# One weight load moved to ScalarE's queue, and two stores moved ahead of GpSimd's casts, in a fused attention and feed-forward kernel

## The chip, the cores and the metric

The kernel runs on one core of a Trainium2 chip. The metric is the device time of one execution in microseconds. Before the change it was 313.09 us, the median of 3 runs (313.03 to 315.12). A profiled execution of the same kernel spans 312.8 us on the core.

The core has five engines with an instruction stream each: TensorE (PE in the profile, its weight loads PEld), VectorE (DVE), ScalarE (ACT), GpSimd (POOL) and SyncE (SP). [...] Transfers between HBM and the core's memory are issued from SyncE's, ScalarE's or GpSimd's stream and carried out by 16 DMA engines.

## The reference, cut to what matters

Sliding-window attention over 8 batches of 8 heads, 576 positions and 64 values per head, followed by two dense layers with a GELU between them. All inputs and the output are float32; the kernel computes in float16 and accumulates in float32.

```python
def attention(q, k, v):                      # (8, 8, 576, 64) each
    scores = q @ k.transpose(0, 1, 3, 2) / 8.0
    pos = np.arange(576)
    mask = np.abs(pos[:, None] - pos[None, :]) <= 32
    scores = np.where(mask, scores, -1e9)
    attn = softmax(scores, axis=-1)          # exp(s - max) / (sum + 1e-9)
    return attn @ v

x = attention(q, k, v).transpose(0, 2, 1, 3).reshape(4608, 512)
h = x @ w_in                                 # (4608, 512) @ (512, 2048)
out = gelu_tanh(h) @ w_out                   # (4608, 2048) @ (2048, 512)
```

## The kernel before

The 4608 rows are worked on in 9 tiles of 512 (`t`), the attention in 8 batches (`b`). While the dense layers of tile `t` run, the attention of batch `t + 1` is woven between their matmuls. Batch 0 has no dense layer to hide behind, so its attention and the loading of the weights make up the start of the kernel.

The start: queries, keys and values of batch 0 are issued on SyncE (two transfers on ScalarE), and after them `w_in`, in four blocks of 512 columns with two halves each (512 KB per half). Of block 0, rows chunks 0 and 1 are the first half.

```python
    def load_w_in(i, w, c0=0, c1=4):
        nc.sync.dma_start(w[:, c0:c1, :], w_in_v[:, c0:c1, 512 * i:512 * i + 512])
        return w
    # ...
    load_table(exp_set)
    vs(4, 0, 1, 2, 3)                        # values of batch 0: tail, then 4 chunks
    wi = []
    for i in range(4):
        wi.append(stage_w())
        for c0 in (0, 2):
            load_w_in(i, wi[i], c0, c0 + 2)
```

The softmax's sums are inverted on ScalarE as exp(-ln(d)), once for each of four groups of heads in batch 0. The first weight block is cast to float16 by GpSimd, ScalarE and VectorE, and TensorE then begins the first dense layer.

```python
    def invert(b, g, d):
        # ... lt: a tile for the result
        nc.scalar.activation(lt[:, 0:n], d[:, 0:n], AF.Ln)
        nc.scalar.activation(lt[:, 0:n], lt[:, 0:n], AF.Exp, scale=-1.0)
        return lt
    # ...
    cast_v(0, 3, nc.vector.tensor_copy)                                       # values, last chunk
    nc.vector.tensor_copy(Vs[0][odd, 7, :, :], Vs[0][odd, 3, :, :])
    nc.scalar.copy(Vs[0][even, 6, :, :], raws[0][3][even, 3, :, :])           # ScalarE's part of it
    for g in range(4):
        times(0, g, os[g], groups.pop((0, g)), (3, 6, 7))                     # weights times values
        spread(0, g, os[g], lts[g])                                           # xT, by the inverted sums
    for c in range(4):
        cast_w(wi[0], w_in16[:, :, 0:512], (3,), (c,), (1,))
```

The end of tile 0: the second dense layer leaves four row blocks (`t4`) of 128 rows. Blocks 0 and 1 go into one tile `yo2`, blocks 2 and 3 into tiles of another pool. They aren't stored at once but put on a list, in the order 0, 3, 1, 2.

```python
        if fc == NF - 1:
            if "yo" not in pys:
                pys["yo"] = hp.tile([128, 2, 512], FP32, name="yo2", tag="qt16")
            yo = pys["yo"][:, t4, :] if t4 < 2 else yp.tile([128, 512], FP32, name="yo", tag="yo")
            (nc.scalar.copy if t4 > 1 else nc.vector.tensor_copy)(yo, pys[t4])
            later.append((t4, yo))
```

The tag `qt16` has one buffer. The next tile of that tag is the float16 tile for the query tails of batch 2, so the first copy into it has to wait until both blocks in `yo2` have been stored. (The profile shortens the tiles' names: `yo` stands for both kinds, and `qt<-qt` is the copy of query tails into `qt16`.)

```python
        def rest(i):                          # query and key tails of batch 2, on ScalarE
            qt16, kt16 = tails_of("q"), tails_of("k") if i == 4 else None
            if i < NPAIR:
                nc.scalar.copy(qt16[:, i, :, :, :].rearrange("p j h d -> p h j d"),
                               qt[:, 2 * i:2 * i + 2, :].rearrange("p h (j d) -> p h j d", j=4))
            # ... i == 3: transpose of the query tails; i == 4: key tails
```

The first dense layer of tile 1 has 16 columns of 128 features (`fc`), each with four matmuls (L530) and a GELU on ScalarE (L538). The stores, the casts of batch 2's values (`cast_v(2, c)`, on GpSimd) and the tail copies (`parts[1]`) stand between them. Three PSUM buffers hold the columns, so TensorE runs at most three columns ahead of the GELUs.

```python
            for fc in range(begun, NF):
                ffn_in(t, fc)                                   # 4 matmuls and the GELU
                if t == 1 and fc == 3:
                    parts[0]()                                  # keys of batch 2; loads of its values
                    combine(4, nc.vector)
                if t == 1 and fc in (5, 6):
                    store(0, *later.pop(0), slice(0, 512), nc.scalar)
                if t == 1 and 6 <= fc < 10:
                    cast_v(2, fc - 6)                           # GpSimd
                if t == 1 and fc == 7:
                    while later:
                        store(0, *later.pop(0))                 # GpSimd
                if t == 1 and 9 <= fc < 14:
                    parts[1](fc - 9)                            # ScalarE: tails
```

After this loop come the second dense layer of tile 1 and, between its matmuls, batch 2's scores, the pairing copies of its values on VectorE (`pair_v`), and the loads of batch 3.

Of the kernel before, what the change touches and what calls it, by code (L numbers as in the profile page):

```python
# [36 lines left out]
def cut(b):  # L37
    return 120 if b else 128
# [33 lines left out]
def kernel(  # L72
# [9 lines left out]
    nc = tc.nc  # L82
# [106 lines left out]
    def pair_v(b, copy, hs=slice(0, H)):  # L189

        V = Vs[b % 2]
        copy(V[64:128, 4:8, hs, :], V[64:128, 0:4, hs, :])
        copy(V[0:64, 4:7, hs, :], V[0:64, 1:4, hs, :])
# [8 lines left out]
    w_in_v = moe_w_in.rearrange("(c p) f -> p c f", p=128)  # L202
    w_out_v = moe_w_out.rearrange("(c p) f -> p c f", p=128)

    def stage_w():
        return stage.tile([128, 4, 512], FP32, name="wst", tag="stage")

    def load_w_in(i, w, c0=0, c1=4):
        nc.sync.dma_start(w[:, c0:c1, :], w_in_v[:, c0:c1, 512 * i:512 * i + 512])  # L209
        return w  # L210

    def load_w_out(i, w, c0=0, c1=4):
# [13 lines left out]
    qk(6)  # L226
    load_table(exp_set)
    vs(4, 0, 1, 2, 3)
    wi = []
    for i in range(4):  # L230
        wi.append(stage_w())
        for c0 in (0, 2):
            load_w_in(i, wi[i], c0, c0 + 2)

    idle = KTs[1][:, 0, 0:512]
    nc.vector.memset(idle, 0.0)
# [57 lines left out]
    def cast_v(b, c, copy=nc.gpsimd.tensor_copy):  # L294
        copy(Vs[b % 2][:, c, :, :], raws[b][3][:, c, :, :])
# [6 lines left out]
    def trans_tails(b, pt, half=slice(0, 128), copy=nc.vector.tensor_copy):  # L302
        t16 = halfs[b][2]
        for pr in range(NPAIR):
            nc.tensor.transpose(pt[:, pr, half], t16[half, 2 * pr:2 * pr + 2, :], idn[half, half])
        if half.stop > 64:
            copy(KLs[b % 2], pt[:, 0:4, 64:128])
        if half.start < 64:
            nc.vector.tensor_copy(QTs[b][:, :, :, 128:144],
                                  pt[:, 0:4, 0:64].rearrange("d r (p j) -> d r j p", j=4))  # L310
# [11 lines left out]
    def trans_out(b, pr, pt, ptk, copy=nc.vector.tensor_copy):  # L322
        nc.vector.tensor_copy(QTs[b][:, pr, :, 0:128], pt[:, 0:4, :])
        copy(
            KTs[b % 2][:, pr, :].rearrange("d (p j) -> d p j", j=4),
            ptk[:, 0:4, :].rearrange("d j p -> d p j"))
# [119 lines left out]
    def sum_up(b, g, d, pe):  # L446
        for h in range(2):
            nc.tensor.matmul(d[64 * h:64 * h + 64, 0:size(b, g)], ones, pe[:, h, :], start=True, stop=True)  # L448
# [15 lines left out]
    def weigh(b, g, pair=None):  # L464
        pe = groups.pop((b, g))
        if pair is not None:
            od = psS.tile([128, 2, 512], FP32, name="ps_od", tag=f"S{pair}")
            o, d = od[:, 0, :], od[:, 1, :]
        else:
            o = psO.tile([128, 512], FP32, name="ps_o", tag="O")  # L470
            d = psO.tile([128, 512], FP32, name="ps_d", tag="D")
        sum_up(b, g, d, pe)
        times(b, g, o, pe)
        return o, d

    def size(b, g):
        return 4 * cut(b) if g < 4 else 4 * NPAIR * (144 - cut(b))

    def invert(b, g, d):
        n = size(b, g)  # L480
        lt = ap_.tile([128, 512], FP32, name="lt") if b or g < 2 or g == 4 else \
            yp.tile([128, 512], FP32, name="lt0", tag="yo")
        nc.scalar.activation(lt[:, 0:n], d[:, 0:n], AF.Ln)  # L483
        nc.scalar.activation(lt[:, 0:n], lt[:, 0:n], AF.Exp, scale=-1.0)  # L484
        return lt

# [24 lines left out]
    def ffn_in(t, n, d0=0, d1=4, then=True):  # L511
        fc = column(t, n)
        if t not in gTs:
            gTs[t] = gp.tile([128, NF, 512], FP16, name="gT", tag="gT")
        if d0 == 0:
            if t == 0:
                i = n % 8
                if i in (4, 6):
                    phs["S"] = psS.tile([128, 2, 512], FP32, name="ph2", tag=f"S{i // 2 - 2}")
                phs[fc] = psO.tile([128, 512], FP32, name="ph", tag="DO"[i]) if i < 2 else \  # L520
                    bank(i - 2) if i < 4 else phs["S"][:, i % 2, :]
            else:
                i = 3 if n in (1, 2) else 0 if n == 0 else (2, 1, 0)[n % 3]
                if n == 1:
                    phs["S"] = psS.tile([128, 2, 512], FP32, name="ph3", tag="S0")
                phs[fc] = bank(i) if i < 2 else phs["S"][:, n - 1, :] if i == 3 else \
                    psO.tile([128, 512], FP32, name="ph", tag="D")
        ph = phs[fc]
        for dc in range(d0, d1):
            nc.tensor.matmul(ph, w_in16[:, dc, fc * 128:fc * 128 + 128],  # L530
                             xT[:, dc, t * 512 % RING:t * 512 % RING + 512],
                             start=(dc == 0), stop=(dc == 3))
        if d1 == 4 and then:
            gelu(t, n)

    def gelu(t, n):
        fc = column(t, n)
        nc.scalar.activation(gTs[t][:, fc, :], phs[fc], AF.Gelu_apprx_tanh)  # L538
        if t and n % 4 == 3:
            sums(t, n // 4)  # L540
# [20 lines left out]
    def combine(i, eng):  # L561
        dst, x, y = wino["todo"][i]
        eng.tensor_tensor(dst, x, y, op=ALU.subtract)
# [14 lines left out]
    def store(t, t4, yo, cols=slice(0, 512), *engs):  # L578

        m = i = 0  # L580
        while m < 128:
            b, c = divmod(t * 512 + t4 * 128 + m, S)
            q0, n = (0, cut(b)) if c < 4 * cut(b) else (cut(b), 144 - cut(b))
            j, p = divmod(c - 4 * q0, n)
            e = min(n - p, 128 - m)
            nj = 1 if p else max(1, min(4 - j, (128 - m) // n))
            eng = engs[i % len(engs)] if engs else nc.gpsimd
            if nj > 1:
                e = nj * n
                eng.dma_start(out_v[b, j:j + nj, q0:q0 + n, cols], yo[m:m + e, cols])  # L590
            else:
                eng.dma_start(out_v[b, j, q0 + p:q0 + p + e, cols], yo[m:m + e, cols])  # L592
            m += e
            i += 1

    later = []
# [84 lines left out]
    def pieces(tag, name):  # L681
        return psO.tile([128, 512], FP32, name=name, tag=tag) if tag in "OD" else \
            psS.tile([128, 2, 512], FP32, name=name, tag=tag)[:, 0, :]

    lts, os = {}, {}

    def sums_of(g):
        d = pieces("DO"[g % 2], "ps_d")
        sum_up(0, g, d, groups[(0, g)])
        lts[g] = invert(0, g, d)  # L690

    cast_early(0, 0, split)
    turn(0)
# [8 lines left out]
    trans_out(0, 1, *pts[1])  # L702
    spin(1)
    sums_of(0)
    cast_early(0, 3, split)
    turn(2)
# [4 lines left out]
    score(0, 2, 0)  # L711
    turn(3)
    trans_out(0, 3, *pts[3])
    sums_of(1)
    score(0, 3, 1)
    sums_of(2)
    cast_v(0, 0)
    cast_v(0, 1)
# [84 lines left out]
    for t in range(NT):  # L803
        b = t + 1
        att = b < B
        if t:
            for fc in range(begun):
                ffn_in(t, fc, 3, 4, then=False)
            for fc in range(begun):
                gelu(t, fc)  # L810
            if att and b > 1:
                parts = cast_and_turn(b)
            for fc in range(begun, NF):
                ffn_in(t, fc)
                if t == 1 and fc == 3:
                    parts[0]()
                    combine(4, nc.vector)
                if t == 1 and fc in (5, 6):
                    store(0, *later.pop(0), slice(0, 512), nc.scalar)
                if t == 1 and 6 <= fc < 10:  # L820
                    cast_v(2, fc - 6)
                if t == 1 and fc == 7:
                    while later:
                        store(0, *later.pop(0))
                if t == 1 and 9 <= fc < 14:
                    parts[1](fc - 9)
                if t == 1 and fc == 8:
                    trans_tails(1, psO.tile([128, 8, 128], FP16, name="pt", tag="O"))
                if t > 1 and fc == 8 and att:
                    pair_v(b, nc.vector.tensor_copy)  # L830
# [10 lines left out]
        for i in range(113 if t else 65):  # L841
# [3 lines left out]
            for act in plan.get(i, "").split():  # L845
                kind, at = act[0], int(act[act.index("@") + 1:]) if "@" in act else None
                g = int(act[1:].split("@")[0])
# [47 lines left out]
                elif kind == "v":  # L895
                    bb, gg = group(g)
                    o, d = weigh(bb, gg, at)
# [51 lines left out]
```

The softmax here doesn't subtract the row's maximum and nothing guards it: scores larger than these inputs give would overflow.

## Time and profile before

| Engine | busy, us | share of the span | instructions |
|---|---|---|---|
| TensorE (matmuls) | 291.1 | 93% | 2894 |
| TensorE (weight loads) | 179.9 | 58% | 2894 |
| VectorE | 194.3 | 62% | 436 |
| ScalarE | 194.2 | 62% | 307 |
| GpSimd | 90.8 | 29% | 140 |

The DMA engines move 50.73 MB, 162 GB/s on average over the span. SyncE's queue carries 37.88 MB of them, GpSimd's 10.83 MB and ScalarE's 1.58 MB.

How to read the views. The page shows the span in 40 equal slices of 7.82 us: for each a digit with the busy share in tenths, a row for the clock granted to TensorE (9 is full, 5 would be half) and a row for the DMA engines. A line of a group of instructions names the line of the kernel, the engine, the operation, what it writes and reads, the count, busy time and mean length in ns, and after the bar the idle time of the engine just before these instructions with what ended most of it. A list of waits gives who waited for what: the total in us, how many times, and the longest. The chain of waits follows back from the last instruction to what released it, step by step. In a timeline a line has a start, a length, the engine, the line of the kernel and the operation; brackets tell of idle time before it and what ended that. A queue (SPq, ACTq, POOLq) is the issuing of a transfer, not the transfer.

### The profile page before, as it was taken

The numbers are of one execution on the slowest core, as the hardware profiler recorded it, in microseconds if no ns is written. First come the engines' busy times: TensorE is split into PE (matmuls) and PEld (weight loads), VectorE is DVE, ScalarE is ACT, GpSimd is POOL, SyncE is SP. The second block draws the span as 40 slices with busy tenths as digits, with TensorE's granted clock in tenths as the row PEclk, the third lists the DMA queues.
The fourth block names the chain that finished last, engine by engine and source line by source line (L and its number), as shares of the span: only waits on it lengthen the run. The fifth ranks groups of instructions, "written<-read, shape, count | busy, mean of one in ns | idle before, by whom it ended". The sixth has DMA issues, their size and how long they took to land.

```text
span 312.8 us, 7121 instructions
## 1 busy us (share of the span) xinstructions
PE 291.1 (93%) x2894; PEld 179.9 (58%) x2894; DVE 194.3 (62%) x436; ACT 194.2 (62%) x307; POOL 90.8 (29%) x140
## 2 busy tenths in 40 slices
PE   7789799980999999999999999999999999999994
PEld 3544344430477448844884587458746874684583
DVE  4663557980395958586758677857785653542452
ACT  4866577641868578657766776677578747805600
POOL 3345426004060605050516042413250041006000
PEclk9999999997699999999999999999999999999999
DMA  7999999998199699989999999969899013004013
GB/s 219 228 340 373 322 280 263 249 224 195 24 250 144 119 168 229 149 138 144 217 160 201 120 243 142 185 131 221 112 132 152 2 30 107 2 0 135 2 34 101
DMA packets 116550, 50.73 MB, mean 162 GB/s; under 512 B 97911, under 2 KB 109943, under 8 KB 116518
## 3 DMA queue, kind: packets, MB, share of 16 engines
q1 hardware_dynamic: 87332, 37.88, 60.4%
q0 software_dynamic: 27776, 10.83, 24.7%
q10 hardware_dynamic: 1410, 1.58, 1.6%
q8 instruction: 22, 0.36, 0.6%
q14 instruction: 10, 0.08, 0.1%
HBM read 36.70 MB, written 9.44 MB: 147 GB/s over the span
## 4 chain that ended last, share of the span: by engine, by line
PE 66%; DMA 20%; SPq 7%; DVE 3%; POOL 1%; issue 1%; ACT 1%; DVEq 0%; ACTq 0%; POOLq 0%
PE mm L628 30%; PE mm L530 15%; PE ph L530 12%; DMA wst<-in_moe_w_out_dram 5%; DMA KT<-k 5%; DMA wst<-in_moe_w_in_dram 4%; PE ps_s L425 3%; SPq L175 2%; PE ps_d L448 2%; SPq L209 2%; SPq L151 2%; DMA tr<-in_k_dram 2%; PE ps_o L458 2%; DMA kr<-in_k_dram 2%; DMA qr<-in_v_dram 1%; DMA out_dram<-yo 1%
## 5 line engine op out<-in xcount | busy, mean ns | idle before, releaser
L530 PEld LDWEIGHTS <-w_in 128*128 128x128 f16 x576 | 56.7, 99 | 77.7 <-issue 12.5
L530 PE MATMUL mm<-xT,w_in 128*128 128x512 f16 x304 | 76.4, 386 | 9.2 <-ACT gT L538 9.1
L538 ACT ACTIVATE gT<-mm 128x512 f16<-128x512 f32 x76 | 45.1, 597 | 40.2 <-PE mm L530 39.5
L530 PE MATMUL ph<-xT,w_in 128*128 128x512 f16 x272 | 69.2, 383 | 0.2
L592 POOL DMA_DIRECT2D out_dram<-y x55 | 32.7, 603 | 87.6 <-DVE y L657 77.2
L573 DVE TENSOR_TENSOR s<-gT 128x512 f16<-128x512 f16 x64 | 26.9, 420 | 48.6 <-ACT gT L538 48.6
L628 PEld LDWEIGHTS <-s 128*128 128x128 f16 x512 | 49.4, 98 | 6.0
L538 ACT ACTIVATE gT<-ph 128x512 f16<-128x512 f32 x68 | 38.0, 600 | 15.0 <-PE ph L530 15.0
L628 PE MATMUL mm<-t,s 128*128 128x256 f16 x376 | 45.1, 273 | 0.0
L628 PEld LDWEIGHTS <-gT 128*128 128x128 f16 x384 | 36.0, 98 | 7.2 <-issue 0.6
L437 ACT ACTIVATE pe<-ps_s 128x960 f16<-128x960 f32 (+1 forms) x32 | 30.4, 975 | 11.8 <-PE ps_s L425 11.7
L628 PE MATMUL mm<-w_out,gT 128*128 128x256 f16 x256 | 33.6, 275 | 0.0
L97 ACT ACT_TABLE_LOAD x17 | 21.8, 1283 | 2.2 <-issue 1.9
L484 ACT ACTIVATE lt<-lt 128x480 f32<-128x480 f32 (+3 forms) x36 | 21.1, 585 | 1.1
L483 ACT ACTIVATE lt<-ps_d 128x480 f32<-128x480 f32 (+2 forms) x28 | 15.5, 555 | 9.0 <-PE ps_d L448 5.1
L443 DVE TENSOR_TENSOR pe<-pe,band 128x960 f16<-128x960 f16 x28 | 18.8, 695 | 1.2 <-ACT pe L437 1.2
L183 POOL DMA_DIRECT2D V<-in_v_dram x20 | 17.9, 910 | 1.1 <-issue 1.1
L458 PEld LDWEIGHTS <-V 128*64 128x64 f16 x520 | 13.9, 111 | 6.4 <-DVE V L200 2.6
L628 PE MATMUL mm<-t,gT 128*128 128x256 f16 x128 | 16.5, 273 | 0.0
L425 PE MATMUL ps_s<-QT,KT 64*64 64x128 f16 (+3 forms) x576 | 13.8, 216 | 0.8 <-DMA KT<-k 0.6
L628 PE MATMUL mm<-w_out,s 128*128 128x256 f16 x120 | 14.4, 273 | 0.0
L573 DVE TENSOR_TENSOR s<-s,gT 128x512 f16<-128x512 f16 x32 | 13.6, 425 | 1.1
(109 smaller groups left out, 320.5 us busy)
## 6 DMA issues: line engine op xcount, KB each, us to landing
kr<-in_k_dram SPq DMA_DIRECT2D x31, 256.0 KB, 10.9
qr<-in_q_dram SPq DMA_DIRECT2D x6, 1024.0 KB
wst<-in_moe_w_in_dram SPq DMA_DIRECT2D x8, 512.0 KB, 9.6
wst<-in_moe_w_out_dram SPq DMA_DIRECT2D x3, 1024.0 KB, 10.9
V<-in_v_dram POOLq DMA_DIRECT2D x20, 128.0 KB, 8.4
vr<-in_v_dram SPq DMA_DIRECT2D x8, 256.0 KB, 5.0
qr<-in_q_dram SPq DMA_DIRECT2D x7, 256.0 KB, 4.3
out_dram<-y POOLq DMA_DIRECT2D x6, 192.0 KB, 6.3
```

The source lines that it names most:

```text
L97: nc.scalar.add_instruction(mybir.InstLoadActFuncSet(name=nc.get_next_instruction_name(), act_func_set_id=which, ins=[], outs=[]))
L183: nc.gpsimd.dma_start(V[:, c, :, :], v[b, :, 128 * c:128 * c + 128, :].rearrange("h p d -> p h d"))
L425: nc.tensor.matmul(ps[64 * half:64 * half + 64, h, 4 * n * r:4 * n * r + 4 * n].rearrange("k (j p) -> k j p", j=4)[:, :, p0 - q0:p1 - q0], ...
L437: nc.scalar.activation(pe, ps[:, :, 0:w], AF.Exp, scale=SCALE)
L443: nc.vector.tensor_tensor(pe, pe, m.rearrange("k (o j) p -> k o j p", o=1).broadcast_to(list(pe.shape)), op=ALU.mult)
L458: nc.tensor.matmul(o[64 * h:64 * h + 64, cols].rearrange("d (j p) -> d j p", j=4)[:, :, p0 - q0:p1 - q0], Vs[b % 2][:, slot, 2 * pr + h, : ...
L484: nc.scalar.activation(lt[:, 0:n], lt[:, 0:n], AF.Exp, scale=-1.0)
L530: nc.tensor.matmul(ph, w_in16[:, dc, fc * 128:fc * 128 + 128], xT[:, dc, t * 512 % RING:t * 512 % RING + 512], start=(dc == 0), stop=(dc = ...
L538: nc.scalar.activation(gTs[t][:, fc, :], phs[fc], AF.Gelu_apprx_tanh)
L573: nc.vector.tensor_tensor(dst, x, y, op=op)
L592: eng.dma_start(out_v[b, j, q0 + p:q0 + p + e, cols], yo[m:m + e, cols])
L628: nc.tensor.matmul(pys["apart"][:, 0:256] if apart else py[:, blk, :], lhsT, wino[w][:, f, :], start=(new and i % (8 if one else 16) == 0) ...
```

## The change

It has two parts.

1. At the start, the first half of the first `w_in` block is issued from ScalarE's stream instead of SyncE's, between the two activations of the second inverse. SyncE issues the other seven halves. The purpose is to have the first half under way beside the loads that are queued on SyncE, instead of behind them.
2. In tile 1's first layer, the two stores of tile 0 that GpSimd issues move ahead of its casts of batch 2's values. They stand behind column 5 instead of column 7, and are taken from the end of the list: block 2, then block 1. ScalarE still stores block 0 behind column 5 and block 3 behind column 6. The purpose is that the stores no longer stand behind casts that have to wait for loads.

No arithmetic is added or removed, and all transfers have the same sizes.

```diff
-    def load_w_in(i, w, c0=0, c1=4):
-        nc.sync.dma_start(w[:, c0:c1, :], w_in_v[:, c0:c1, 512 * i:512 * i + 512])
+    def load_w_in(i, w, c0=0, c1=4, queue=nc.sync):
+        queue.dma_start(w[:, c0:c1, :], w_in_v[:, c0:c1, 512 * i:512 * i + 512])
         return w
 ...
     vs(4, 0, 1, 2, 3)
-    wi = []
-    for i in range(4):
-        wi.append(stage_w())
-        for c0 in (0, 2):
-            load_w_in(i, wi[i], c0, c0 + 2)
 ...
-    def invert(b, g, d):
+    def invert(b, g, d, between=lambda: None):
 ...
         nc.scalar.activation(lt[:, 0:n], d[:, 0:n], AF.Ln)
+        between()
         nc.scalar.activation(lt[:, 0:n], lt[:, 0:n], AF.Exp, scale=-1.0)
 ...
-    def sums_of(g):
+    def sums_of(g, *between):
         d = pieces("DO"[g % 2], "ps_d")
         sum_up(0, g, d, groups[(0, g)])
-        lts[g] = invert(0, g, d)
+        lts[g] = invert(0, g, d, *between)
+
+    wi = []
+
+    def load_all_w_in():
+        for i in range(4):
+            wi.append(stage_w())
+            for c0 in (0, 2):
+                load_w_in(i, wi[i], c0, c0 + 2, nc.sync if i or c0 else nc.scalar)
 ...
-    sums_of(1)
+    sums_of(1, load_all_w_in)
 ...
                 if t == 1 and fc in (5, 6):
                     store(0, *later.pop(0), slice(0, 512), nc.scalar)
+                if t == 1 and fc == 5:
+                    while len(later) > 1:
+                        store(0, *later.pop())
                 if t == 1 and 6 <= fc < 10:
                     cast_v(2, fc - 6)
-                if t == 1 and fc == 7:
-                    while later:
-                        store(0, *later.pop(0))
```

## The prediction

> **What bounds the kernel now.** I read the page first. TensorE is busy 93% of the span, and from 96 us on nearly every 6 us stretch of the table by stretches is full. Time lost once ahead of that stays lost, so I looked for a hole in TensorE, and the page points at one place: the granted clock dips once, over two slices, the DMA engines run nearly dry in the second of them, and nearly all idle time of one group of matmuls has one cause.
>
> ```profile
> PEclk9999999997699999999999999999999999999999
> DMA  7999999998199699989999999969899013004013
> L530 PE MATMUL mm<-xT,w_in 128*128 128x512 f16 x304 | 76.4, 386 | 9.2 <-ACT gT L538 9.1
> ```
>
> A slice is 7.82 us, so the 7 and the 6 of the clock row are 70.4 to 86.0 us. Next, the waits in the window 56 to 90 us (total, times, longest):
>
> ```profile
> POOL V L295 <- DMA qr<-in_v_dram: 17.3, 2, 16.5
> DVE s L573 <- ACT gT L538: 13.9, 2, 10.5
> ...
> ACT qt L359 <- DMA out_dram<-yo: 9.9, 1, 9.9
> PE mm L530 <- ACT gT L538: 9.1, 1, 9.1
> ```
>
> TensorE waits 9.1 us for a GELU of ScalarE, and ScalarE stands 9.9 us ahead of a copy of query tails, waiting for a *store*. The chain that ended last, in the window 53 to 90 us, says which (start, length):
>
> ```profile
> 69.26 4.24 DMA qr<-in_v_dram
> ...
> 73.62 0.55 POOL V L295
> 74.17 2.99 DMA out_dram<-yo
> 77.23 0.62 ACT qt L359
> 77.85 0.50 ACT gT L538
> 78.39 3.57 PE mm L530 x8
> ```
>
> Read upwards: GpSimd waited for the values of batch 2, cast two chunks, and only then issued the stores of tile 0. The store is of `yo2`, whose memory the query-tail tile `qt16` takes over. The timeline shows that the data had been ready for long:
>
> ```profile
> 58.66 0.68 DVE L608 COPY yo<-mm 128x512 f32<-128x512 f32 x1
> 63.10 0.37 ACTq L592 DMA_DIRECT2D out_dram<-yo  x1
> 72.14 0.61 POOL L295 CAST V<-qr 128x512 f16<-128x512 f32 x1 [16.47 <-DMA qr<-in_v_dram]
> 74.17 1.29 POOL L592 DMA_DIRECT2D out_dram<-yo  x2
> 83.70 0.60 ACT L538 ACTIVATE gT<-ph 128x512 f16<-128x512 f32 x1 [1.11 <-PE ph L530]
> ```
>
> The second half of `yo2` was complete at 59.34 us (58.66 + 0.68); GpSimd, idle from 55.67, issued its store some 15 us later. The last line is the last GELU of tile 1, done at 84.30: the mark I count from.
>
> For the first part of the change, the start (queue instructions are marked SPq):
>
> ```profile
> 12.02 6.25 SPq L209 DMA_DIRECT2D wst<-in_moe_w_in_dram  x8
> 13.21 0.63 ACT L484 ACTIVATE lt<-lt 128x512 f32<-128x512 f32 x1
> 18.93 6.60 PEld L530 LDWEIGHTS <-w_in 128*128 128x128 f16 x32 [0.60 <-POOL w_in L218]
> 26.04 4.86 PEld L530 LDWEIGHTS <-w_in 128*128 128x128 f16 x24 [0.51 <-DVE w_in L218]
> ```
>
> TensorE enters the first layer at 18.93 behind a cast of the first weight block, and stops again at 26.04 behind a later block. Throughout, the DMA engines' share of the stretches lies at 0.99 to 1.14 (12 to 36 us; it counts overlapping packets, so full is about 1).
>
> **What the Trainium skill says.** "DMA: Bandwidth & Descriptors", Issuing engines are not separate DMA queues: transfers issued from different engines run on the same 16 DMA engines, and another issuer saves only the issue time. The trace agrees as far as it goes: with the engines full from 4 us on, I give part one no bandwidth. The same page, Anatomy of one DMA: a semaphore wait happens on the issuing sequencer, before dispatch. That is the defect here: a store queued behind casts that wait for a load waits with them (16.47 us). "TensorE: Matmul & The Clock Gate", What's actually happening: after an idle window of about 3.4 us the array's clock halves until it has been busy for about as long. The trace agrees: after 9.12 us of idleness the granted clock is 0.50 in 78 to 82 us, and eight matmuls of L530 take 3.57 us where a later row has 1.73.
>
> **Part two, the stores, step by step.** GpSimd now has the two stores ahead of the casts and in reverse order: row block 2 (from `yp`, ready at 58.19) and row block 1 (in `yo2`, ready at 59.34). Nothing is added or removed; blocks 0 and 3 stay on ScalarE.
> 1. GpSimd is free, so both are issued by about 60 us (0.56 and 0.74 us each, allowing some delay beside a busy VectorE), and the one that matters lands at about 63 to 64 (3.0 us from issue to landing before; I allow 4).
> 2. The copy of query tails then waits for the *other* store into `yo2`'s memory, ScalarE's at 63.10. ScalarE's stores took 4.8 us to land: 63.10 + 4.8 = 67.9. ScalarE itself gets there at 67.31 (its GELU at 66.71 takes 0.60). So it resumes at about **68.0 instead of 77.23: 9.2 us earlier**, with 0.7 us of wait left.
> 3. Five tail copies and six GELUs remain. Before, they took 84.30 - 77.23 = 7.07 us, of which the end waited for TensorE at half clock (1.11 us before the last). Now TensorE does not go cold: it ends its filled buffers at 69.27, and the first GELU frees one at about 69.2. A column is then 4 x 0.216 = 0.86 us, while a copy and a GELU together come every 1.00 us (77.23, 78.25, 79.24, 80.24). So ScalarE sets the pace: five pairs at 1.00, the sixth GELU and its start, about 5.9 us. The last GELU ends at about 68.0 + 5.9 = **73.9 instead of 84.30: 10.4 us earlier**.
> 4. What follows hangs on that GELU: the second layer of tile 1, the exp table, and batch 2's scores. Later stretches have TensorE 6.00 of 6.00 busy, so I carry the 10.4 us to the end.
>
> **What moves against it.** The stores now go through the DMA engines at 59 to 64 us, where their share is 0.97 to 1.21, not at 74 to 78, where it is 0.57. In the window 56 to 80 us GpSimd's queue moved these same 0.52 MB in 5.9% of 16 engines' time: 0.059 x 24 = 1.4 us. Everything queued behind may land that much later. Does it meet TensorE?
> - Keys of batch 2: the second transpose is issued at 67.70 and transposes took 4.0 us: 71.7, or 73.1 delayed. The scores stood at 85.03 and would come at 74.6. Clear by 1.5 us.
> - Values of batch 2: GpSimd's casts ended at 76.63, with 1.29 us of store issue among them. Minus 1.29, plus 1.4: 76.7. VectorE's pairing copies came at 88.93 and would come at 78.5. Clear by 1.8 us.
> - Batch 3's loads started at 84.96 and move forward with the rest, into the hole that the DMA row shows (share 0.02 in 78 to 82).
> So I book 0 here, with up to 2 us of risk.
>
> **Part one, the weight block.** One issue (0.47 us in most rows, 2.48 for the first) leaves SyncE and goes to ScalarE between the two activations of the second inverse, at about 13.2. SyncE's next seven move up by one place. ScalarE is busy 3.94 of 4.00 us in 12 to 16, so the issue may push its later work, the value cast at 16.95 included, by about 0.5 us, and with it the first matmul at 18.93. Against this, the first half no longer queues behind the last value chunk, so some of the 0.60 us wait may go. Either way TensorE stops at 26.04 for weights whose bytes and engines are unchanged, and this hides most of the difference. I book **0, within 0.4 either way**.
>
> Sum: 313.09 - 10.4 + 0 = **302.7 us**.
>
> **Rivals.**
> - *Another wait takes its place.* The tail copy also needs its load, issued at 59.88 behind four key loads of some 8 us; or the value loads slip more than I think, and VectorE stands at the pairing copies. For it: DMA share above 1 from 62 to 74. Against: margins of 1.5 us and more. It would leave 6 to 9 us of gain: 304 to 307.
> - *ScalarE's own store lands late*, since GpSimd's now precede it in busy DMA engines: the remaining wait grows from 0.7 to 2 us or so: about 304.
> - *The gain is given back later*, because DMA bounds the steady state (share up to 1.93 at 156 to 162 us). Against it: TensorE waits for keys only 0.6 us in total from 100 to 245 us. If it were so, the gain would be near 5 us: 308.
> - *Part one decides*, faster or slower by over 1 us. Against: the stop at 26.04, and full DMA engines before and after.
>
> **Range and chances.** A best case, with the store landing before 67.3 and 0.5 us from part one, is a gain of about 12: 301. A late store and 2 us of new waits leave 7 to 8: 305.8. So 301.0 to 305.8. Two per cent is 6.3 us; only the rival that gives back later, or a new wait of over 4 us, would hide that. Faster 0.93, within two per cent 0.06, slower 0.01.
>
> **What would show it.** After the change: GpSimd's store issues at 58 to 61 us; the wait of the tail copy for a store below 2 us; no wait of 9 us of L530 on GELU; no dip in the clock row near 70 to 86; the last GELU of tile 1 at 73 to 75; the score matmuls of batch 2 at 74 to 76 with no wait on transposes; the same lengths per tile after that. For part one: an ACTq load at about 13.2 and a first matmul of L530 between 18.5 and 19.5. Wrong would be: a long idle time of ScalarE at the tail copy under another name, or of TensorE or VectorE at the scores or the pairing copies.

## The result, and the profile after

The changed kernel takes 304.43 us, the median of 4 runs (304.10 to 306.82), against 313.19 us for the kernel before (median of 4). The ratio is 0.972, with a 95% interval of 0.966 to 0.979: 8.8 us less, with the interval between 6.7 and 10.6. The prediction was 302.7 us in a range of 301.0 to 305.8. A second measurement of the same kernel beside another set of runs gave 0.973 (0.968 to 0.977).

The same three rows of the page, of the kernel after (its lines are numbered 4 lower from the first layer on: L526 is L530 of before, L534 is L538, L354 is L359, L588 is L592):

```profile
PEclk9999999997999999999999999999999999999999
DMA  7999999999797999698989997989596031004013
L526 PE MATMUL mm<-xT,w_in 128*128 128x512 f16 x304 | 75.7, 382 | 2.5 <-ACT gT L534 2.4
```

The stop of TensorE at the GELU is down from 9.1 to 2.4 us, and the hole in the DMA row is gone. But the clock row still has a 7 in the slice from 68 us on: the stop is shorter, and a stretch at a lower clock still followed it (0.62 on average in 70 to 74 us). The waits in the window 56 to 90 us (total, times, longest) say what is left of it:

```profile
POOL V L290 <- DMA qr<-in_v_dram: 16.6, 4, 14.4
...
ACT qt L354 <- DMA out_dram<-yo: 3.2, 1, 3.2
POOL out_dram L588 <- ACT yo L604: 2.4, 1, 2.4
PE mm L526 <- ACT gT L534: 2.4, 1, 2.4
...
DVE k L368 <- DMA kr<-in_k_dram: 1.5, 1, 1.5
```

GpSimd still waits long for the values, but nothing is queued behind that any more: its stores now wait only for their data. ScalarE's wait for a store is 3.2 us, not 9.9. New is the last line: VectorE waits for key loads, which it did not do in this window before. The timeline shows the stores (the lines with DMA_DIRECT2D are issues):

```profile
56.80 0.74 POOL L588 DMA_DIRECT2D out_dram<-yo  x1 [2.44 <-ACT yo L604]
...
57.96 0.55 POOL L588 DMA_DIRECT2D out_dram<-yo  x1 [0.41 <-DVE yo L604]
...
61.41 0.37 ACTq L588 DMA_DIRECT2D out_dram<-yo  x1
...
64.31 1.43 DVE L368 CAST k<-kr 128x512 f16<-128x512 f32 x4 [1.51 <-DMA kr<-in_k_dram]
...
68.81 0.62 ACT L354 CAST qt<-qt 16x512 f16<-16x512 f32 x1 [3.19 <-DMA out_dram<-yo]
...
74.57 0.60 ACT L534 ACTIVATE gT<-ph 128x512 f16<-128x512 f32 x1 [0.67 <-PE ph L526]
...
75.56 0.40 PE L420 MATMUL ps_s<-QT,KT 64*64 64x96 f16 x16
```

GpSimd's stores went out as soon as there was something to store. Both of them precede ScalarE's at 61.41, and it is *this* one that the tail copy now waits for. The chain of waits has it as one step, the longest in this window:

```profile
61.41 7.30 DMA out_dram<-yo
...
68.81 0.62 ACT qt L354
```

7.30 us from issue to landing, where the slowest of tile 0's stores took 4.8 before. What the store did in that time can be read from the DMA queues (packets, MB, share of 16 engines; q1 is SyncE's queue, q10 ScalarE's, q0 GpSimd's). In 62 to 66 us of the kernel after:

```profile
q1 hardware_dynamic: 2117, 0.61, 129.1%
q10 hardware_dynamic: 9, 0.02, 1.1%
```

Of ScalarE's two stores, issued at 61.41 and 62.27, almost nothing moved before 66 us; in 66 to 69 us q10 moved 0.51 MB. The kernel before has the same picture: its two were issued at 63.10 and 63.96, moved nothing before 66 us and 0.52 MB in 66 to 69. What differs is SyncE's queue ahead of them: in 58 to 62 us it moved 0.80 MB before, and 0.47 MB after, beside 0.51 MB of GpSimd's stores. As far as these totals tell, GpSimd's early stores took room from SyncE's transfers, and ScalarE's store moved when those had run down.

A profile is one execution, and that of the kernel before was one of its longer ones (314.56 us), so the two spans, 312.8 and 302.4, lie further apart than the medians. I compare stages, by five marks that can be read in every timeline: the last cast of `w_in`; ScalarE's table load at the end of tile 0; the first tail copy; the table load right after the last GELU of tile 1; and the one near the end of tile 1's second layer, with the span.

| kernel | last w_in cast | end of tile 0 | tail copy | after last GELU | second layer | span |
|---|---|---|---|---|---|---|
| before | 29.68 | 58.21 | 77.23 | 84.32 | 100.88 | 312.8 |
| after | 28.23 | 56.52 | 68.81 | 75.19 | 91.28 | 302.4 |
| part two only | 29.57 | 58.20 | 71.25 | 77.14 | 92.54 | 304.2 |
| part one only | 28.40 | 56.62 | 75.70 | 82.12 | 98.08 | 309.3 |
| block 0 on GpSimd | 28.61 | 57.20 | 66.25 | 71.83 | 90.91 | 302.5 |
| block 2's store late | 28.54 | 57.04 | 68.56 | 74.15 | 89.73 | 301.4 |
| only two stores early | 28.43 | 56.73 | 65.72 | 71.29 | 87.28 | 298.3 |

From before to after, 1.7 us are gained by the end of tile 0, 6.7 more up to the tail copy, 0.7 between it and the last GELU, 0.5 in the second layer and 0.8 later. The medians lie only 8.8 us apart, so that some of the last steps may be the spread of single executions.

### The profile page after: what moved, and what is told of

It is laid out like the page before. It is cut to its first block, busy times and chain, and to the rows that moved or that the text cites. A ratio compares the mean times of both kernels' runs of the same rounds, so it can differ in the third digit from the quotient of the medians.

```text
span 302.4 us, 7119 instructions
## 1 busy us (share of the span) xinstructions
PE 289.5 (96%) x2894; PEld 179.7 (59%) x2894; DVE 194.5 (64%) x436; ACT 194.2 (64%) x307; POOL 90.4 (30%) x140
## 4 chain that ended last, share of the span: by engine, by line
PE 82%; DMA 9%; DVE 4%; ACT 2%; issue 0%; POOL 0%; SPq 0%; DVEq 0%; ACTq 0%
PE mm L624 32%; PE mm L526 20%; PE ph L526 17%; DMA wst<-in_moe_w_out_dram 3%; PE ps_s L420 3%; DMA out_dram<-yo 2%; PE ps_d L443 2%; DMA wst<-in_moe_w_in_dram 2%; PE ps_o L453 2%; DMA tr<-in_k_dram 2%; PE mm L598 2%; PE py L598 1%; PE ps_od L443 1%; DVE t L559 1%; DVE xT L489 1%; ACT pe L432 1%
## 5 line engine op out<-in xcount | busy, mean ns | idle before, releaser
L526 PEld LDWEIGHTS <-w_in 128*128 128x128 f16 x576 | 56.5, 98 | 70.3 <-issue 5.0
L526 PE MATMUL mm<-xT,w_in 128*128 128x512 f16 x304 | 75.7, 382 | 2.5 <-ACT gT L534 2.4
L534 ACT ACTIVATE gT<-mm 128x512 f16<-128x512 f32 x76 | 45.1, 597 | 40.0 <-PE mm L526 39.2
L526 PE MATMUL ph<-xT,w_in 128*128 128x512 f16 x272 | 69.1, 383 | 0.2 <-POOL w_in L218 0.2
L588 POOL DMA_DIRECT2D out_dram<-y x55 | 33.0, 609 | 85.8 <-DVE y L653 77.3
L534 ACT ACTIVATE gT<-ph 128x512 f16<-128x512 f32 x68 | 38.0, 600 | 14.2 <-PE ph L526 14.2
L432 ACT ACTIVATE pe<-ps_s 128x960 f16<-128x960 f32 (+1 forms) x32 | 30.4, 975 | 10.7 <-PE ps_s L420 10.6
L847 POOL COPY after<-KL 128x1 f16<-128x1 f16 x5 | 1.1, 227 | 43.8 <-DMA KL<-kt 43.8
## 6 DMA issues: line engine op xcount, KB each, us to landing
wst<-in_moe_w_out_dram SPq DMA_DIRECT2D x3, 1024.0 KB, 10.6
```

Source lines behind the costliest of these rows:

```text
L432: nc.scalar.activation(pe, ps[:, :, 0:w], AF.Exp, scale=SCALE)
```

## The experiments

My theory after the result: part one does bring something (about 1.5 us, against 0 predicted), and part two brings less than predicted, as ScalarE's own store lands late behind GpSimd's. The rivals: the start's difference is only spread between executions; the transposes make the store late; or this stage is bound by batch 2's loads anyway.

**Each part alone.** Part two on the kernel before:

```diff
@@ before @@
                     store(0, *later.pop(0), slice(0, 512), nc.scalar)
+                if t == 1 and fc == 5:
+                    while len(later) > 1:
+                        store(0, *later.pop())
 ...
-                if t == 1 and fc == 7:
-                    while later:
-                        store(0, *later.pop(0))
```

> The kernel before, with the stores moved and the weight load left on SyncE. Theory A (the profile of the changed kernel reached its first table load of tile 1 1.7 us earlier because of the load on ScalarE's queue, 56.52 against 58.21): this kernel has the old start, with that table load at 57.5 to 58.2, and gains only what the stores give, about 7.4 us up to the last GELU of tile 1: a time of 305 to 306.5. Rival B (the 1.7 us are the spread between executions, and part one is worth nothing): the same time as the changed kernel, 304.4 within 0.5.

Measured: 305.86 us, ratio 0.974 (0.970 to 0.978), which is 8.2 us of 313.9. Its start is that of the kernel before to about 0.1 us in both marks, as theory A has it. Its store of block 0 landed 8.07 us after the issue:

```profile
63.09 8.07 DMA out_dram<-yo
```

Part one alone (the changed kernel with the stores put back behind the casts):

> The changed kernel with the stores put back behind the casts, so that only the load on ScalarE's queue is new. Theory A: the first table load of tile 1 comes about 1.5 us earlier than in the kernel before (56.5), but the wait of the tail copy for the store behind the value casts swallows some of it, as the value loads set that store's time: 311.5 to 313. Rival B: no difference from the kernel before in any stage, 313.1 within 0.4.

Measured: 312.54 us, ratio 0.9957 (0.9937 to 0.9977): 1.4 us, between 0.7 and 2.0. The gain of the start arrives at the tail copy almost undiminished, 75.70 against 77.23, as in this version the chain there begins with the loads. So part one is not nothing. On top of part two it can't be told from the medians, 0.974 and 0.972 to 0.973 with intervals of 0.004 to 0.006 either way; it is the marks of the start that show it: with one half on ScalarE's queue in time, tile 0 ends at 56.5 to 57.2 in every profile, without it at 58.2.

**Where part one's gain comes from.** The stretches 12 to 16 and 16 to 20 us (busy time and instructions per engine, then TensorE's clock, the DMA engines' share and GB/s). First of the kernel before:

```profile
12.00:16.00 4.00, 2.75 (x57) 1.44 (x55) 1.83 (x5) 3.94 (x7) 1.38 (x3) 1.00 1.09 198
16.00:20.00 4.00, 3.09 (x49) 1.50 (x48) 3.09 (x8) 3.42 (x5) 1.43 (x3) 1.00 0.99 297
```

And of the kernel after:

```profile
12.00:16.00 4.00, 2.56 (x55) 1.33 (x53) 1.59 (x5) 3.94 (x7) 1.41 (x3) 1.00 1.26 253
16.00:20.00 4.00, 3.04 (x49) 1.49 (x48) 3.11 (x8) 3.13 (x5) 1.47 (x3) 1.00 1.02 346
```

In these 8 us 0.42 MB more were moved: 4 x (55 + 49) = 416 KB, which is 1.2 us at 346 GB/s. All the later weights come earlier by about that: the last cast of `w_in` comes at 28.1 to 28.6 us in seven profiles with an early load on ScalarE's queue, at 29.6 and 29.7 in the two without.

By single microseconds, the gain begins where SyncE's value loads, in pieces of 256 bytes, run out. In 12 to 14 us the two kernels moved 222 and 224 GB/s, and ScalarE's queue nothing yet. In the three microseconds from 14 to 17 it was 166, 182 and 239 GB/s before, and 237, 328 and 385 after. The middle one, before and then after:

```profile
15.00:16.00 1.00, 1.00 (x26) 0.62 (x23) 0.00 (x0) 0.97 (x3) 0.16 (x1) 1.00 0.65 182
15.00:16.00 1.00, 1.00 (x27) 0.58 (x20) 0.00 (x0) 0.97 (x2) 0.19 (x1) 1.00 1.01 328
```

With a share of 0.65, the DMA engines had room there that SyncE's queue alone did not use. To see whether it is the company of the value loads that counts, the same half block was issued from ScalarE later, at the fourth inverse:

```diff
@@ after @@
-    sums_of(1, load_all_w_in)
+    sums_of(1, load_w_in_sync)          # the seven halves on SyncE
 ...
-    sums_of(3)
+    sums_of(3, load_w_in_act)           # the first half of block 0, on ScalarE
```

> The changed kernel with the same half block on ScalarE's queue, but issued at the fourth inverse (about 15.8 us) instead of the second (12.3 us). Theory G (the gain of part one is that a second queue works beside SyncE's value loads, which are cut into pieces of 256 bytes; these are through by about 16 us): the rate in 12 to 16 us falls back to about 200 GB/s, the weights' last casts come at 29.5 again instead of 28.2, the first table load of tile 1 at 57.5 to 58.2, the time at 305.5 to 306. Rival L (what counts is that SyncE has one transfer fewer to issue): the later weights come as early as in the changed kernel, and the time is 304.4.

Measured: 308.40 us, ratio 0.985 (0.981 to 0.988), slower even than part two alone. The rates are 203 and 249 GB/s, as theory G had it for the first. What I had not reckoned with: issued at 16.54 us behind SyncE's halves, this half was there for the casts only some 9 us later, and the whole first layer waited for it:

```profile
16.54 0.41 ACTq L209 DMA_DIRECT2D wst<-in_moe_w_in_dram  x1
...
25.84 5.32 POOL L218 CAST w_in<-wst 128x512 f16<-128x512 f32 x8 [9.40 <-DMA wst<-in_moe_w_in_dram]
...
26.51 0.13 PEld L526 LDWEIGHTS <-w_in 128*128 128x128 f16 x2 [7.31 <-POOL w_in L218]
```

So the time of this run can't be set against part one's. Its rates say less than I had hoped, too: the half moved nothing before 20 us (in 16 to 20 us all 0.99 MB went by SyncE's queue), and SyncE's first weight issue had slipped by 1 us, to 13.07. When the half did move, in 20 to 24 us, the rate was 395 GB/s against 396 in the kernel before: there the second queue brought nothing. That the pieces of 256 bytes are the reason is not shown. One place fewer in SyncE's line brought at most a part: the last cast of `w_in` came 17.2 us after SyncE's first weight issue (30.27 - 13.07), against 16.2 in the kernel after (28.23 - 12.00) and 17.7 before (29.68 - 12.02). Then the other direction, both halves of the block on ScalarE's queue:

```diff
@@ after @@
-                load_w_in(i, wi[i], c0, c0 + 2, nc.sync if i or c0 else nc.scalar)
+                load_w_in(i, wi[i], c0, c0 + 2, nc.sync if i else nc.scalar)
```

> The changed kernel with both halves of the first weight block on ScalarE's queue instead of one. Theory E (a second queue lets the DMA engines move more in 12 to 20 us, when SyncE's queue holds loads in pieces of 256 bytes: 253 and 346 GB/s against 198 and 297 in the kernel before): another 0.3 to 1 us earlier at the first table load of tile 1, 303.5 to 304.2, or the last value chunk comes later and takes it back. Rival F (only the place in SyncE's order counts; the engines were full): no difference from the changed kernel, 304.4 within 0.4.

Measured: 303.62 us, ratio 0.965 (0.960 to 0.970), which overlaps with the changed kernel's. The rates, 258 and 350 GB/s, are those with one half: here the second added nothing. It also had a price: the first issue took 0.37 us at 12.42, beside the Ln, and delayed nothing; the second took 1.40 us and held the Exp up by 1.19. TensorE entered the first layer at 20.52, after 18.95 and 19.88 in the changed kernel's two profiles, at a clock of 0.51 in 20 to 24 us, and tile 0 ended at 59.39, over 2 us later than in either, where theory E had it up to 1 us earlier. That the time is nevertheless no longer comes from the next stage: its tail copy ran at 68.63, 0.2 us ahead of the changed kernel's. The next experiments say why.

**The late store.** The marks of part two alone say that the late landing of this store is the main difference to the prediction. The most direct test is to give ScalarE nothing to wait for: both blocks of the shared tile on GpSimd, early, and 2 and 3 on ScalarE.

```diff
@@ after @@
-                if t == 1 and fc in (5, 6):
-                    store(0, *later.pop(0), slice(0, 512), nc.scalar)
                 if t == 1 and fc == 5:
-                    while len(later) > 1:
-                        store(0, *later.pop())
+                    store(0, *later.pop(0))
+                    store(0, *later.pop(1))
+                if t == 1 and fc in (5, 6):
+                    store(0, *later.pop(), slice(0, 512), nc.scalar)
```

> The changed kernel, with the stores of the two blocks in the shared tile (0 and 1) both on GpSimd, ahead of its casts, and blocks 2 and 3 on ScalarE. Theory C (what is left of the tail copy's wait, 3.19 us, is the 7.3 us that ScalarE's late store needs to land, and TensorE's second dip of the clock follows from it): the wait vanishes, TensorE stays at full clock, the last GELU of tile 1 ends at 71.5 to 72.5 instead of 75.17; part of it may be lost again to the value loads, whose casts end at 77.8 where the pairing copies would want them at 75.7: 301.5 to 303.5. Rival D (the transposes or the value loads of batch 2 bound this stage in any case): the wait moves to the scores or the pairing copies, and the time stays at 304 within 0.5.

Measured: 304.45 us, ratio 0.969 (0.965 to 0.973). The store's wait is gone, the tail copy comes at 66.25 and the table load after the last GELU at 71.83: 3.4 us earlier than in the changed kernel, though it had left tile 0 0.7 us later. Yet the next mark is only 0.4 us earlier, and the time is the same within the intervals. What took it back stands in the waits of the window 68 to 92 us:

```profile
PEld L453 <- DVE V L193: 2.5, 1, 2.5
DVE V L192 <- POOL V L290: 2.4, 1, 2.4
PE ps_od L453 <- DVE V L193: 2.2, 1, 2.2
```

VectorE's pairing copies wait for GpSimd's casts of the values, and TensorE for the copies; its clock then was 0.80 in 78 to 82 us. Rival D was right in this stage: behind the store stood the values of batch 2, about as late, and without them the earlier tail copy did not pay.

Is the store late because of the other stores? Block 2's store, which nothing waits for, behind the casts instead:

```diff
@@ after @@
                 if t == 1 and fc == 5:
-                    while len(later) > 1:
-                        store(0, *later.pop())
+                    store(0, *later.pop(1))
                 if t == 1 and 6 <= fc < 10:
                     cast_v(2, fc - 6)
+                if t == 1 and fc == 9:
+                    store(0, *later.pop())
```

> The changed kernel, but GpSimd stores only block 1 ahead of its casts, and block 2 (which nothing waits for) behind the last of them. Theory H (the store that the tail copy waits for lands slowly, 7.3 us against 4.8, because GpSimd's 512 KB go through the same DMA engines just before it): with 256 KB less in 57 to 62 us that store lands in 5.5 to 6.5 us, the wait of the tail copy shrinks from 3.2 to about 2 us, and the key loads land about 0.7 us earlier: 303.5 to 304. Rival I (the transposes of the queries, issued about 1.4 us before the store, make it slow): the store takes over 7 us as before, 304.4.

Measured: 303.00 us, ratio 0.968 (0.964 to 0.972). The store of block 0 landed at most 6.2 us after its issue at 62.22, as theory H expected, and TensorE's clock stayed full. The keys' casts started at 64.01, 7.0 us after the end of tile 0 instead of 7.8.

```profile
68.56 0.62 ACT L354 CAST qt<-qt 16x512 f16<-16x512 f32 x1 [2.13 <-DVE QT L304]
```

The bracket of this line names a copy of VectorE (68.15 to 68.56), but in the run with block 0 on GpSimd the tail copy ran at 66.25, ahead of that copy of VectorE's (68.66 there): it is not what the tail copy needs. The store, landed by about 68.5, fits.

But GpSimd's stores alone do not make it slow. In the run with two halves on ScalarE's queue all four stores were early too, in the same order and at the same distances (GpSimd's at 59.68 and 60.83), and there block 0's landed in 4.3 us:

```profile
64.28 4.26 DMA out_dram<-yo
```

The stores came 2.9 us later than in the changed kernel, and SyncE's queue had got further: ScalarE's two stores moved nothing in 62 to 66 us and all their 0.52 MB in 66 to 69, the same microseconds as in the kernels before and after. So the time to landing is mostly the time until SyncE's earlier transfers have run down, and GpSimd's stores count as far as they hold those up.

Finally both together: blocks 0 and 1 on GpSimd early, 2 and 3 on GpSimd behind the casts, nothing on ScalarE.

```diff
@@ after @@
-                if t == 1 and fc in (5, 6):
-                    store(0, *later.pop(0), slice(0, 512), nc.scalar)
                 if t == 1 and fc == 5:
-                    while len(later) > 1:
-                        store(0, *later.pop())
+                    store(0, *later.pop(0))
+                    store(0, *later.pop(1))
                 if t == 1 and 6 <= fc < 10:
                     cast_v(2, fc - 6)
+                if t == 1 and fc == 9:
+                    while later:
+                        store(0, *later.pop(0))
```

> The two blocks in the shared tile (0 and 1) are stored by GpSimd ahead of its casts, blocks 2 and 3 by GpSimd behind the last cast, and nothing by ScalarE: half of the store traffic leaves the full DMA engines. Theory J (with the tail copy's wait gone, the values of batch 2 bound this stage, and they come late because stores, key loads and transposes share the DMA engines): the casts of the values end 1 to 1.5 us earlier than in the run with all four stores early (77.6 to 78.2), the wait of VectorE at the pairing copy shrinks from 2.4 to about 1 us: 302.5 to 303.5. Rival K (the values come late because SyncE issues them behind the transposes, whatever the traffic): they end at 77.5 and the time stays at 304.4.

Measured: 300.69 us, ratio 0.961 (0.957 to 0.966), and 0.961 (0.957 to 0.965) when it was run again. Beside the same runs the changed kernel had 305.12:

> The changed kernel itself again, on the same chip and beside the same runs of the kernel before as the other three, so that they can be compared with it: 304.4 within 0.6, and the first table load of tile 1 at 56.5 to 57.2, as in the runs with part one.

This version beats both kernels, by 12.0 and by 4.4 us, more than theory J had (302.5 to 303.5 us). With 0.52 MB of stores out of the way, GpSimd's casts of the values end at 75.89 (73.88 + 2.01) instead of 78.22, and VectorE hardly waits for them:

```profile
75.93 0.42 DVE L192 COPY V<-V 64x1024 f16<-64x1024 f16 x1 [0.51 <-POOL V L290]
```

The value loads themselves were no faster: from their first issue to the end of the last cast it took 8.8 us here (from 67.06) and 8.1 with block 0 on GpSimd (from 70.12). They were issued 3.1 us earlier, because SyncE was through with the transposes ahead of them earlier. Rival K had that order right, but not that the values would come as late whatever the traffic.

The last pair of runs sets this version with two halves of the weight block on ScalarE's queue beside the same with one:

> The version with only the two needed stores early (blocks 0 and 1 on GpSimd ahead of the casts, 2 and 3 behind them) and, as well, both halves of the first weight block on ScalarE's queue. Theory M (one half already fills what the value loads leave free: 12 to 16 us moved 258 GB/s with two halves and 253 to 260 with one; and the second issue held ScalarE up for 1.2 us): no gain over the same kernel with one half, within 0.6 us, or up to 1 us slower. Rival N (each half beside the value loads brings over a microsecond): another 1 us faster, 299.7.

> The version with only the two needed stores early and one half on ScalarE's queue, again, beside the same runs as the one with two halves: 300.7 within 0.8, and 0.961 of the kernel before.

Measured: 302.19 us (0.962, 0.958 to 0.967) with two halves and 301.36 with one. Theory M holds; there is no more to be had from a second half. Again tile 0 ended 2.9 us later with two (59.83 against 56.90).

## Why the prediction was right, and where it was off

The time lies in the range, and the cause was the predicted one: the stores no longer stand behind casts that wait for loads. That it lies so close is in part luck, as two errors offset each other. By the prediction's steps:

1. *GpSimd's stores at 58 to 61 us*: right in kind; at 56.80 and 57.96, as tile 0 ended 1.7 us earlier. They landed 4.7 to 5.0 us after issue; I had allowed 4.
2. *ScalarE resumes at 68.0, 9.2 us earlier, with 0.7 us of wait left*: this is the step that failed. In part two alone it resumed at 71.25, 6.0 us earlier. The mis-sized term is the landing of ScalarE's store. I took 4.8 us from the profile before, where GpSimd's stores were not in the DMA engines, as if it were a property of the store. It took 7.3 and 7.6 us in two profiles of the changed kernel, 8.1 in part two alone, 6.2 with 256 KB of stores fewer ahead of it, and 4.3 where all came later: it moved when SyncE's transfers had run down. That was my second rival, "ScalarE's own store lands late", with about 304 us; the measured time is its time.
3. *5.9 us from the tail copy to the last GELU, ScalarE at 1.00 us a pair*: in part two alone 71.25 to 77.13, 5.88 us; after, 68.81 to 75.17, 6.4. The pace of ScalarE's pairs, 1.00 us, was right. *TensorE does not go cold*: wrong, a consequence of step 2. It stopped 2.4 us and the stretch 70 to 74 has a clock of 0.62. Two of the signs that I had named thus failed: a wait below 2 us at the tail copy (3.19) and no dip of the clock.
4. *The gain is carried to the end*: right. In the two profiles the spans lie 10.4 us apart and the last GELUs 9.1; by the medians, 8.8 apart, at most a few tenths were given back, as far as one pair of profiles can tell.

*What moves against it*: the stores delayed the key loads enough that VectorE waited 1.5 us for them; I had put at most 1.4 us on everything queued behind. The margins I gave the keys and values held in the changed kernel, at the pace its late store left: its scores came at 75.56 without a wait, and the casts of the values ended at 77.78, just before the pairing copies at 79.04. At the pace I had predicted the values would have been the next wait, as block 0 on GpSimd shows. So a store that landed on time would not have brought the whole 10.4 us either: two limits stood close together, and I had looked at the second with numbers from a profile without the stores.

*Part one, 0 within 0.4*: off; it is 1.4 us alone. The failing step is "with the engines full from 4 us on, I give part one no bandwidth". I read the DMA engines' share of 1.09 in 12 to 16 us as full. With the second queue it was 1.26, and over a quarter more was moved; within those 4 us there was a microsecond with a share of 0.65. I also expected the issue at 13.2 us and half a microsecond of delay for ScalarE; it went out at 12.27, and the Exp began at 12.97, no later than before. The two errors, 1.4 us too little for part one and 2.2 too much for part two (10.4 against 8.2), have opposite signs and leave 0.8 us. The measured gain was 1.6 us below the forecast; the other 0.8 us lie within the interval of the result.

The Trainium skill's "DMA: Bandwidth & Descriptors", Issuing engines are not separate DMA queues, on which I rested that step, says that another issuer saves only issue time. I took that to be worth nothing, and the moved load brought 1.4 us. Whether more than issue time was saved, no run here shows: SyncE's first weight issue took 2.48 us in the kernel before (12.02 to 14.50), ScalarE's 0.37 us at 12.27.

What stays open: why the second queue helps in 14 to 17 us. That it saves SyncE's long issue is one explanation, the change from pieces of 256 bytes to pieces of 2 KB another; no run separates them. Open, too, is by which mechanism ScalarE's store stays behind SyncE's transfers, and how much of these are transposes and how much key loads.

## What to carry to other kernels

What stands behind a waiting instruction in an engine's stream waits with it: here a store that was ready at 59.34 us was issued at 74.17, and GELUs stood behind a copy that waited 9.9 us. Look for stores and frees queued behind casts that depend on a load, and put them where their data is ready. Advance only the transfers that something waits for, though: here two stores that nothing waited for, moved out of the busy stretch, were worth about 0.8% of the time (0.969 to 0.961, from two sets of runs). And when a wait goes away, look for the next dependency due in the same microseconds, with its time as it will be under the new traffic, not as it was in the old profile.

## What the runs showed of the hardware that I had not expected

- The time from issue to landing of one and the same 256 KB store depends on what else is under way: 3.0 us for GpSimd's at 74 us (before), and for ScalarE's store of block 0 4.8 (before), 7.3 (after) and 4.3 (two halves). The share of the DMA engines does not tell it: in 62 to 66 us it was 1.21, 1.31 and 1.07, but with part one alone it was 1.27 and the store took 4.9.
- A transfer on ScalarE's queue can stand behind those that SyncE has issued before it: ScalarE's stores, issued at 61.41 and 62.27, moved 0.02 MB before 66 us, and a half block issued at 16.54 us moved nothing before 20 us.
- A mean share of about 1 is not a full DMA system: over 12 to 16 us it was 1.09 before, with 0.65 in one of these microseconds; with a second queue it was 1.26, and the rate went from 198 to 253 GB/s.
- Single executions of one kernel differ by 2 to 4 us (300.02 to 303.87 with only two stores early). Several profiles of these kernels show a granted clock of 0.5 to 0.7 somewhere in 16 to 24 us and others none. The repeated profile of the changed kernel has it (0.70 in 16 to 20 us) and is 1.3 us longer than the first.
